# A third of the K of `h @ w_out` as seven block products, in a kernel of windowed attention and two gated layers

## The chip, the cores and the metric

One core of one Trainium2 chip. The metric is device time of one execution in microseconds (us); lower is better.

## What is computed

```
scores = q @ k.T / sqrt(64), masked to 0 <= row - col < 64; x = softmax(scores) @ v
h   = silu(x @ w_gate) * (x @ w_val)
x2  = h @ w_out
out = ((x2 @ w1) * (x2 @ w2)) @ w3 @ w_out2
```

q, k, v have 4 batches, 8 heads, 576 rows and 64 columns; x is taken as 2304 tokens of 512. w_gate and w_val are 512x1536, w_out 1536x512, w1 and w2 512x1024, w3 1024x1024, w_out2 1024x512. All of it is fp32. The results of attention feed the first gated layer, and so on to the end: it is one chain.

## The kernel before

**Words and passes.** Every fp32 operand is split into a high word and the rest (`cast` makes the first, `rest` the second), and every product is made in three passes over the words: high by high, high by low, low by high (`PASSES`). One matmul takes a weight tile of 128x128 and 384 token columns.

**Stages.** TensorE (PE) works through attention, the first gated layer (36 units), the projection by w_out (`project`, matmuls at L834), the second gated layer, and last the product with w3 and w_out2, which are multiplied with each other on the way. The 2304 tokens are three parts (`tp`) of 768, each in two halves of 384 columns.

**A gated unit** (`Unit.product`) makes one 256-column group (`fp`) of one weight (x = 0: gate, x = 1: value) for one token part as seven block products in place of eight: sums of the operands' blocks are made first, and sums of the products afterwards. A product is 6 matmuls. The banks of PSUM that it goes through are named `al`, `ga`, `be`; in a trace their names end in a and b for x = 0 and 1, and the operand words are `xo` (first layer) and `xp` (second). DVE makes the sums (`add`, `combine`, L681, L231) and the rests (L227), ACT the copies out of PSUM (L377) and the casts (L218), and the finished group of h goes to HBM as `h`.

**The projection** is the plain product: for each token part 12 tiles of K, and for each of them 4 tiles of output columns, 2 token halves and 3 passes, 288 matmuls. The 8 sums (4 by 2) stay in the 8 banks of PSUM (`o`). Nothing but the words of h (`pl` and `ph`, loaded back from HBM by `Rows.queue` 384 KB at a time, then cast and rest) and the resident tiles of w_out (`wo`) is waited for. In the last tile of K each bank is evicted as it is done (`evict`, on ACT L377 and L817, on DVE L820). ACT and DVE also narrow and split weights that are needed later (`st_z`, `st_w`, `st_a`: `narrow`, L194 to L207), and SP writes their words to HBM (`zd`, `w3d`).

**The order on the other engines.** A planner (`Plan`) writes it while the kernel is built. Work is a `Job` with a rank, a due number, costs and a lag; `fill` puts into an engine's stream whatever could start by its reckoning, `need` puts a job there because the next matmul reads it. What stands in a stream is done in that order: an instruction that waits holds up all that stands behind it on its engine. All loads of the projection are issued by SP, and eight DMA semaphores go round, so each DMA waits for the eighth before it.

## Time and profile before

| | |
|---|---|
| median of 3 runs | 825.1 us (824.4 to 825.12) |
| profiled execution, span | 822.8 us |
| PE busy | 811.8 us |
| the projection | from 362.02 to 511.78 us of the span |

The profile is of one execution, and shows its span, from the first instruction to the last; the page gives no other time for that execution. The median lies 2.3 us above the span, which is what a run has around the instructions. Busy time of PE is a sum over the pipelined matmuls; whether it stands still is read from its waits and from the distance of matmul starts, not from the busy share.

### The profile page before, as it was taken

The numbers are of one execution on the slowest core, as the hardware profiler recorded it, in microseconds if no ns is written. First come the engines' busy times: TensorE is split into PE (matmuls) and PEld (weight loads), VectorE is DVE, ScalarE is ACT, GpSimd is POOL, SyncE is SP. The second block draws the span as 40 slices with busy tenths as digits, with TensorE's granted clock in tenths as the row PEclk, the third lists the DMA queues.
The fourth block names the chain that finished last, engine by engine and source line by source line (L and its number), as shares of the span: only waits on it lengthen the run. The fifth ranks groups of instructions, "written<-read, shape, count | busy, mean of one in ns | idle before, by whom it ended". The sixth has DMA issues, their size and how long they took to land.

```text
span 822.8 us, 15571 instructions
## 1 busy us (share of the span) xinstructions
PE 811.8 (99%) x5702; PEld 783.5 (95%) x5702; DVE 637.4 (77%) x1353; ACT 455.1 (55%) x1194; POOL 90.8 (11%) x135
## 2 busy tenths in 40 slices
PE   7999999999999999999999999999999999999998
PEld 5777899999999999999999999999999998899997
DVE  5899898686887959866888683877888844789994
ACT  6899997555556445633663551444444423655543
POOL 3666842000000000000000000000010110000000
PEclk9999999999999999999999999999999999999999
DMA  9999295253562444599987712024565289107632
GB/s 187 195 200 197 46 238 113 90 192 129 192 222 79 148 154 179 210 360 403 373 264 175 231 57 103 29 83 134 166 205 157 108 295 325 37 3 207 182 71 78
DMA packets 172765, 140.23 MB, mean 170 GB/s; under 512 B 120848, under 2 KB 142608, under 8 KB 171664
## 3 DMA queue, kind: packets, MB, share of 16 engines
q1 hardware_dynamic: 167888, 125.86, 50.6%
q0 software_dynamic: 4800, 13.37, 5.9%
q8 instruction: 45, 0.74, 0.4%
q14 instruction: 32, 0.26, 0.1%
HBM read 92.27 MB, written 42.99 MB: 164 GB/s over the span
## 4 chain that ended last, share of the span: by engine, by line
PE 91%; ACT 4%; SPq 2%; DMA 2%; DVE 1%; issue 0%; POOL 0%; ACTq 0%
PE o L834 18%; PE ala L669 15%; PE alb L669 15%; PE bea L669 8%; PE beb L669 8%; PE acc L992 5%; PE al L1135 4%; PE gaa L669 4%; PE gab L669 4%; ACT pexp L480 2%; PE be L1135 2%; PE al L1067 2%; PE PV L519 1%; SPq L403 1%; PE be L1067 1%; PE ga L1135 1%
## 5 line engine op out<-in xcount | busy, mean ns | idle before, releaser
L834 PE MATMUL o<-ph,wo 128*128 128x384 f32 x576 | 146.2, 334 | 0.0
L834 PEld LDWEIGHTS o<-ph,wo 128*128 128x128 f32 x576 | 103.9, 188 | 0.0
L834 PE MATMUL o<-pl,wo 128*128 128x384 f32 x288 | 96.2, 334 | 0.0
L377 ACT ACTIVATE ha<-ala 128x384 f32<-128x384 f32 x102 | 49.5, 489 | 50.1 <-PE ala L669 49.5
L759 POOL DMA_DIRECT2D h<-ha x24 | 13.0, 544 | 548.2 <-DVE ha L691 548.2
L681 DVE TENSOR_TENSOR ha<-ha,bea 128x384 f32<-128x384 f32 x60 | 33.1, 551 | 38.5 <-PE bea L669 22.1
L834 PEld LDWEIGHTS o<-pl,wo 128*128 128x128 f32 x288 | 54.1, 188 | 0.0
L480 ACT ACTIVATE pexp<-S,stat 128x128 f32<-128x128 f32 x144 | 53.3, 428 | 0.0
L218 ACT CAST hf<-h 128x384 fp32r<-128x384 f32 x84 | 38.7, 514 | 14.4 <-DVE h L231 13.6
L694 ACT ACTIVATE ha<-ha 128x384 f32<-128x384 f32 x54 | 28.3, 526 | 32.4 <-DVE ha L681 32.4
L227 DVE TENSOR_TENSOR hf<-h,hf 128x384 fp32r<-128x384 f32 x84 | 42.2, 545 | 4.9 <-ACT hf L218 4.8
L227 DVE TENSOR_TENSOR pl<-pl,ph 128x768 fp32r<-128x768 f32 x36 | 33.4, 953 | 13.2 <-ACT ph L218 12.8
L218 ACT CAST ph<-pl 128x768 fp32r<-128x768 f32 x36 | 29.2, 837 | 25.1 <-DMA pl<-h 22.6
L490 POOL TENSOR_TENSOR pexp<-pexp,stat 128x384 f32<-128x384 f32 x48 | 39.0, 833 | 36.4 <-DVE stat L487 18.0
L377 ACT ACTIVATE c12b<-alb 128x384 f32<-128x384 f32 x30 | 14.8, 493 | 50.3 <-PE alb L669 50.0
L480 ACT ACTIVATION_READ_ACCUMULATOR pexp<-S,stat 128x1 f32 x144 | 38.1, 267 | 0.0
L681 DVE TENSOR_TENSOR c22b<-c22b,beb 128x384 f32<-128x384 f32 x30 | 16.6, 553 | 25.8 <-ACT c22b L377 25.8
L669 PE MATMUL ala<-xo,w_g_7h 128*128 128x384 f32 x120 | 30.3, 336 | 0.5 <-ACT ha L377 0.5
L473 DVE TENSOR_REDUCE stat<-S 128x3 f32<-128x384 f32 x48 | 24.4, 550 | 7.6 <-PE S L466 7.4
L669 PE MATMUL ala<-xo,w_g_1h 128*128 128x384 f32 x126 | 29.2, 335 | 0.0
L218 ACT CAST xp<-X 128x384 fp32r<-128x384 f32 x42 | 19.7, 519 | 10.9 <-DVE X L231 8.0
L377 ACT ACTIVATE c11b<-alb 128x384 f32<-128x384 f32 x30 | 14.7, 489 | 19.5 <-PE alb L669 19.5
(625 smaller groups left out, 2453.2 us busy)
## 6 DMA issues: line engine op xcount, KB each, us to landing
h<-ha SPq DMA_DIRECT2D x36, 384.0 KB, 3.0
pl<-h SPq DMA_DIRECT2D x36, 384.0 KB, 6.3
h<-ha POOLq DMA_DIRECT2D x24, 384.0 KB, 3.2
h<-h SPq DMA_DIRECT2D x24, 384.0 KB, 6.4
st_w<-in_moe_w_dram SPq DMA_DIRECT2D x8, 1024.0 KB, 6.5
st_wo<-in_moe_w_out_dram SPq DMA_DIRECT2D x6, 1024.0 KB, 5.1
wo<-by_wo SPq DMA_DIRECT2D x12, 512.0 KB, 4.1
st_g<-in_moe_w_gate_dram SPq DMA_DIRECT2D x5, 1024.0 KB, 5.2
```

The lines of the kernel that those rows point to most:

```text
L218: (eng.copy if eng is nc.scalar else eng.tensor_copy)(out=hi(), in_=src())
L227: return plan.job(lambda eng: eng.tensor_tensor(out=lo(), in0=src(), in1=hi().bitcast(F32), op=ALU.subtract), after, slots=slots, due=due, ...
L377: nc.scalar.mul(out=out, in_=in_, mul=-1.0)
L480: nc.scalar.activation(out=pe[:, jj, :], in_=so[:, jj, :], func=AF.Exp, bias=st[:, 0, x, jj:jj + 1], accum_out=st[:, 1, x, jj:jj + 1])
L490: nc.gpsimd.tensor_tensor(out=pe, in0=pe, in1=st[:, 3, x, :].unsqueeze(2).to_broadcast([P, SUB, P]), op=ALU.mult)
L669: nc.tensor.matmul(acc, lhsT=self.wt.ops[p, x][:, m, :], rhs=self.xs.ops[p, m][:, y, :], start=start and n == 0, stop=n == 5, skip_group_c ...
L681: nc.vector.tensor_tensor(out=out, in0=x, in1=y, op=ALU.add)
L694: nc.scalar.activation(out=h, in_=src, func=func, scale=-1.0 if direct else 1.0)
L834: nc.tensor.matmul(acc[m, x], lhsT=wos.tiles[i // 6][:, i % 6, :], rhs=rows[2 * tp + x].words(f, b), start=f == n == 0, stop=f == NF - 1 a ...
L992: nc.tensor.matmul(acc, lhsT=w3T[i][c // 3][:, x, (c % 3) * P:(c % 3) * P + P], rhs=zt[c, y], start=c == k == 0, stop=c == NI - 1 and k == 2)
L1067: nc.tensor.matmul(acc, lhsT=self.xs.ops[p, m][:, x, t * P:t * P + P], rhs=right.ops[p, m, y], start=start and n == 0, stop=n == 3 * R - 1 ...
L1135: nc.tensor.matmul(acc, lhsT=right.ops[p, m, y][:, P * k:P * k + P], rhs=self.xs.ops[p, m][:, x, :], start=bool(name) and n == 0, stop=n = ...
```

## The change

**Seven products for a third of K.** In the projection the K groups 0 and 1 (512 of 1536) are taken as a 2x2 block product with seven products (`SEVEN`, `STEPS`), the other four groups stay plain. Per token part that is 7 x 2 x 2 x 3 = 84 matmuls in place of 96, and 276 in place of 288. The seven come first in each part. Their banks are used again inside the part: after product 1 ACT copies `al` to `ga` (`seed`), after product 6 it copies `al` out, after product 7 it copies `al` to `de`; the plain groups then add onto `al`, `be`, `ga` and `de`.

**The operands of the seven.** The sums of h are made by DVE at the end of the units of value groups 0 and 1 (`spread`: four adds, and six stores by SP in place of two). Those of w_out are made in the class `Seven` (seven operands for each group). The projection loads 15 pairs of rows for each part in place of 12, and w_out lies in 20 resident tiles in place of 16.

**With it.** From the seventh unit on, gated units copy the first product into the bank of the second one, which adds onto it (`AT_SEEDED`): one DVE add less per unit. `narrow` handles weights that come in one load in pieces of 1024 columns in place of two of 512. The planner gets counts of rows, due numbers for loads, and shorter lags; the pool `half` has 5 buffers in place of 7, `sl` 58 in place of 56.

```diff
+AT_SEEDED = {1: 0, 5: 2, 2: 3, 6: 4, 7: 8, 4: 12, 3: 13}
...
@@ -137,7 +145,7 @@
                     for j in self.queue:
                         if e not in j.cost or (j.early and e == "DVE" and not self.early) or any(x.done is None for x in j.after):
                             continue
-                        if j.slots and self.slots < j.slots + self.keep:
+                        if j.slots and self.slots < j.slots + self.keep or j.rows and (self.rows[j.rows] < 1 or j.behind and j.behind.done is None):
                             continue
                         at = max([t] + [x.done for x in j.after])
...
 
-        n = 512
         a = plan.job(lambda eng: eng.tensor_scalar(out=low(), in0=low(), scalar1=29, scalar2=None,
                                                    op0=ALU.logical_shift_right), [load], due=due,
...
+    def cast(hi, src, after, n, slots=1, negate=False, due=0.0, rows=0):
         def fn(eng):
             if negate and eng is nc.scalar:
...
+            if self.second is None:
+                return [narrow(lambda: self.st, self.loaded[0], self.due, 1024)] * 2
+            return [narrow(lambda j=j: self.st[:, 512 * j:512 * j + 512], self.loaded[j], self.due, 512) for j in range(2)]
 
         def make(self):
             pass
...
+    SEEDED = 6
+    SEVEN = (0, 1)
+    stored = {}
...
+                elif (i, t) == (0, 0) and self.seeded:
+                    nc.scalar.copy(out=h, in_=src)
+                    plan.charge("ACT", act(T))
 
...
+
+
+                    self.seeded = self.n >= SEEDED
+                    if self.seeded:
+                        self.ga = bank(f"ga{self.name}")[:, :T]
+                    self.c11 = self.ga if self.seeded else self.own(0, 0, "c11")
                     later(1, lambda: self.copy(self.c11, self.al))
+                elif p == 2 and self.seeded:
+                    plan.wait(self.read)
+                    self.mm(self.ga, 2)
+                    self.put(0, 0, self.ga)
                 elif p == 2:
-                    ga = bank(f"ga{self.name}")[:, :T]
-                    self.mm(ga, 2, True)
-                    self.add(self.c11, self.c11, ga)
+                    self.ga = bank(f"ga{self.name}")[:, :T]
+                    self.mm(self.ga, 2, True)
+                    self.add(self.c11, self.c11, self.ga)
...
-                            store(out=hd[self.fp, self.tp][:, i, :], in_=t)
-                        plan.slots += 2
+                        h = hs.pop((self.fp, self.tp))
+                        if func != AF.Copy and self.fp in SEVEN:
+                            spread(self.fp, self.tp, h)
+                        else:
+                            for i, t in enumerate(h):
+                                store(out=hd[self.fp, self.tp][:, i, :], in_=t)
+                            plan.slots += 2
+                            done = mark()
+                            done.done = plan.charge("DVE", 0.0) + 4.0
+                            stored[self.fp, self.tp] = [done]
...
+    H_AT = {1: 0, 5: 1, 2: 2, 3: 3, 6: 4, 7: 5, 4: 6}
...
+    def spread(fp, tp, h):
+
+
+        to, f = h7d[tp], SEVEN.index(fp)
+        keep, plan.rank = plan.rank, SPREAD_RANK
+        (h00, h01), (h10, h11) = ((t[:, :T], t[:, T:]) for t in h)
...
+        first = put((1,), lambda: h00, [now])
+        both = put((2, 3), lambda: h[1].rearrange("p (c t) -> p c t", c=2), [now])
+        extra = []
+
+        def apart():
+            extra.append(small([P, T], F32, f"hs{fp}_{tp}"))
+            return extra[0]
+        s7 = combine(apart, lambda: h01, lambda: h11, ALU.add, [now], T)
+        s5 = combine(lambda: h01, lambda: h01, lambda: h00, ALU.add, [s7], T)
+        s6 = combine(lambda: h11, lambda: h11, lambda: h01, ALU.add, [s5, both], T)
+        s4 = combine(lambda: h10, lambda: h10, lambda: h11, ALU.add, [s6], T)
+        p5 = put((5,), lambda: h01, [s5])
+        put((7,), lambda: extra[0], [s7])
+        put((6,), lambda: h11, [s6])
+        p4 = put((4,), lambda: h10, [s4])
+        plan.job(gone, [first, p5, s6], SP=0.0)
+        plan.job(gone, [p4], SP=0.0)
+        plan.rank = keep
+
+
...
 
...
-                eng.dma_start(out=self.lo[fp].bitcast(F32), in_=self.hd[fp, self.tp][:, :, T * self.x:T * self.x + T])
+                self.lo[key] = slot([P, 2, T], F32R, f"pl{self.tp}_{key[0]}_{key[1]}", False)
+                f, x = key
+                eng.dma_start(out=self.lo[key].bitcast(F32),
+                              in_=h7d[self.tp][:, H_AT[f]] if x == 7 else h1d[f, self.tp][:, :, T * x:T * x + T])
 
             def hi():
-                self.hi[fp] = slot([P, 2, T], F32R, f"{self.name}h{self.tp}_{self.x}_{fp}")
-                return self.hi[fp]
-            a = loading(load, after, 2)
-            b = cast(hi, lambda: self.lo[fp].bitcast(F32), [a], 2 * T)
-            self.jobs[fp] = rest(lambda: self.lo[fp], lambda: self.lo[fp].bitcast(F32), lambda: self.hi[fp], [b], 2 * T)
-
-        def words(self, f, x):
-            return (self.lo if x else self.hi)[f // 2][:, f % 2, :]
+                self.hi[key] = slot([P, 2, T], F32R, f"ph{self.tp}_{key[0]}_{key[1]}", False)
+                return self.hi[key]
+            a = loading(load, stored[key[0], self.tp, 7] if key[1] == 7 else stored[key[0], self.tp], rows=1, lag=7.0, due=due)
...
+    STEPS = (1, 5, 6, 2, 7, 3, 4)
...
-            acc = {(m, x): bank(f"o{tp}_{m}_{x}")[:, :T] for m in range(NM) for x in range(2)}
-
-            def evict(m, x):
-
-
-                dst = x2[m][:, T * x:T * x + T]
-                if x or tp == 0:
...
+            al, ga, be, de = ([None] * 2 for _ in range(4))
+            r = rows[tp]
+
+            def open_bank(to, m, name):
+                to[m] = bank(f"{name}{tp}_{m}")[:, :T]
+
+            def seed(to, src, m, name):
+                open_bank(to, m, name)
+                nc.scalar.copy(out=to[m], in_=src[m])
+                plan.charge("ACT", act(T))
...
+            def copy(r, c, src, m):
+                (negated if r == c else nc.scalar.copy)(out=part(r, c, m), in_=src[m])
+                plan.charge("ACT", act(T))
+
+            def add(r, c, src, op, m):
+                nc.vector.tensor_tensor(out=part(r, c, m), in0=part(r, c, m), in1=src[m], op=op)
+                plan.charge("DVE", dve(T))
+
+            def product(acc, key, w, g, m, start=False, stop=False):
+                plan.need(r.jobs[key])
+                for n, (x, y) in enumerate(PASSES):
+                    plan.need(wos.job(w, g, x, m))
+                    nc.tensor.matmul(acc, lhsT=wos.words(w, g, x, m), rhs=r.words(key, g, y),
+                                     start=start and n == 0, stop=stop and n == 2, skip_group_check=not start)
...
+            for k, p in enumerate(STEPS):
+                for event in events.get((tp, k), ()):
...
+                to = {2: ga, 5: be, 3: be}.get(p, al)
+                for m in range(2):
+                    if p in (1, 5):
+                        open_bank(to, m, "al" if p == 1 else "be")
+                    for g in range(2):
+                        product(to[m], (p, 7), p, g, m, p in (1, 5) and g == 0, True)
+                    if p == 1:
+                        seed(ga, al, m, "ga")
+                    elif p == 5:
+                        copy(1, 1, be, m)
+                    elif p == 6:
+                        copy(0, 1, al, m)
+                    elif p == 7:
+                        seed(de, al, m, "de")
+                    if m:
...
+            for k, fp in enumerate(plain):
+                for event in events.get((tp, len(STEPS) + k), ()):
+                    event()
+                for g in range(2):
+                    last = g == 1 and fp == plain[-1]
+                    for b, (i, c, to) in enumerate(((1, 0, al), (0, 1, be), (0, 0, ga), (1, 1, de))):
+                        for m in range(2):
+                            product(to[m], (fp, c), (fp, i), g, m, False, last)
+                            if last:
+                                if (i, c) == (1, 0):
+                                    copy(1, 0, al, m)
+                                elif (i, c) == (0, 1):
+                                    add(0, 1, be, ALU.add, m)
+                                elif (i, c) == (0, 0):
+                                    copy(0, 0, ga, m)
+                                else:
+                                    add(1, 1, de, ALU.subtract, m)
+                        if b == 1 or b == 3:
...
+            xop2[tp] = Operands([lambda x=x: x for x in x2], f"xp{tp}", dict.fromkeys(PRODUCTS, opened), X2_SUMS, X2_RESTS, due=14.0 * tp)
...
+    class Seven(Doubles):
+
+
+        GROUPS = ((1, 2), (5, 6), (7, 3), (4,))
+
+        def __init__(self, src, n):
+            super().__init__(src[256 * n:256 * n + 256, :].rearrange("(j p) f -> p j f", p=P), f"wo{n}")
...
+
+                def put(eng, group=group, t=t):
+                    for q, p in enumerate(group):
+                        eng.dma_start(out=w7d[p][:, SEVEN.index(self.n)], in_=t[0][:, q].rearrange("p x f -> p (x f)").bitcast(F32))
+                by.append(plan.job(put, jobs, lag=5.0, SP=0.5 * len(group)))
+                for p in group:
+                    self.stored[p] = by[-1]
...
+    on(events1, last1 - 2, lambda: (make_to(wo[-1]), weight_loads(0, 4)))
+    on(events1, last1 - 1, lambda: (share(), project_loads(0), weight_loads(4, 7)))
+    on(events1, last1, lambda: weight_loads(7, 9))
     events_p = {}
-    on(events_p, (0, 0), lambda: (setattr(plan, "landing", 10.0), make_to(w3s[NW3 - 1])))
+    on(events_p, (0, 0), lambda: (setattr(plan, "landing", 8.0), setattr(plan, "keep", 0), make_to(w3s[NW3 - 1])))
+    for n in range(3):
+        on(events_p, (0, 2 * n), lambda n=n: weight_loads(9 + 2 * n, 11 + 2 * n))
+    on(events_p, (0, 7), lambda: project_loads(1))
+    on(events_p, (1, 7), lambda: project_loads(2))
+    opened = mark()
+    X2_SUMS, X2_RESTS = (), ()
...
```

**How it moves instructions, 1: DVE in the first gated layer, at the end of the unit of value group 0, first token part (about 123 us in the trace of before).** `X2_0` and `X2_1` hold columns of x of the third token part, `xo2_50` to `xo2_61` its operand words for products 5 and 6, `ha` and `c11b`, `c22b` the sums of the units, `st_g1` a weight that is narrowed. Before:

```order
L691 TENSOR_TENSOR ha0_1_0_2330<-ha0_1_0_2330,c11b0_1_2428 128x384
L227 TENSOR_TENSOR xo2_50_2462<-X2_0_1540,xo2_50_2462 128x384
L227 TENSOR_TENSOR xo2_51_2472<-X2_1_1632,xo2_51_2472 128x384
L231 TENSOR_TENSOR X2_0_1540<-X2_0_1540,X2_2_1794 128x384
L231 TENSOR_TENSOR X2_1_1632<-X2_1_1632,X2_3_1879 128x384
L681 TENSOR_TENSOR ha0_1_0_2330<-ha0_1_0_2330,bea0_1_2374 128x384
L194 TENSOR_SCALAR st_g1_2253<-st_g1_2253 128x512
L227 TENSOR_TENSOR xo2_60_2506<-X2_0_1540,xo2_60_2506 128x384
L227 TENSOR_TENSOR xo2_61_2509<-X2_1_1632,xo2_61_2509 128x384
```

Now, from the third of the four added sums of h (`ha0_0_1`) on:

```order
L238 TENSOR_TENSOR ha0_0_1_2125<-ha0_0_1_2125,ha0_0_0_2124 128x384
L238 TENSOR_TENSOR X2_1_1642<-X2_1_1642 128x384
L238 TENSOR_TENSOR ha0_0_1_2125<-ha0_0_1_2125 128x384
L695 TENSOR_TENSOR ha0_1_0_2340<-ha0_1_0_2340,bea0_1_2384 128x384
L201 TENSOR_SCALAR st_g1_2263<-st_g1_2263 128x1024
L234 TENSOR_TENSOR xo2_50_2519<-X2_0_1550,xo2_50_2519 128x384
L234 TENSOR_TENSOR xo2_51_2522<-X2_1_1642,xo2_51_2522 128x384
L238 TENSOR_TENSOR X2_0_1550<-X2_0_1550,X2_2_1804 128x384
L695 TENSOR_TENSOR c22b0_1_2543<-c22b0_1_2543,beb0_1_2477 128x384
L702 SCALAR_TENSOR_TENSOR ha0_1_1_2341<-c22b0_1_2543,ha0_1_1_2341 128x384
L695 TENSOR_TENSOR ha0_2_0_2525<-ha0_2_0_2525,gaa0_2_2550 128x384
L234 TENSOR_TENSOR xo2_60_2559<-X2_0_1550,xo2_60_2559 128x384
```

The words `xo2_50` and `xo2_51` stood ahead of the add to `ha0_1_0` and of the narrowing; now they stand behind both, and the narrowing is twice as wide. `xo2_60` has moved behind three instructions of the units (`c22b`, `ha0_1_1`, `ha0_2_0`) that stood behind it. The sum that makes `X2_1` stood ahead of `xo2_60`; it now follows right behind the last row, and `xo2_61` behind it.

**2: ACT at the change from the first to the second token part of the projection (about 412 us).** `X2` are the results that leave PSUM, `ph1` the high words of the second part's rows, `st_w30` and `st_w31` pieces of w3. Before:

```order
L203 ACTIVATE st_w30_5228<-st_w30_5228 128x512 x2
L377 ACTIVATE X2_0_0_4932<-o0_0_0_4936 128x384
L817 COPY X2_0_0_4932<-o0_0_1_4937 128x384
L377 ACTIVATE X2_0_1_4933<-o0_1_0_4938 128x384
L817 COPY X2_0_1_4933<-o0_1_1_4939 128x384
L817 COPY X2_0_2_4934<-o0_2_0_4940 128x384
L377 ACTIVATE X2_0_2_4934<-o0_2_1_4941 128x384
L817 COPY X2_0_3_4935<-o0_3_0_4942 128x384
L377 ACTIVATE X2_0_3_4935<-o0_3_1_4943 128x384
L218 CAST ph1_0_1_5387<-pl1_0_1_5297 128x768
```

Now:

```order
L225 CAST ph1_6_7_5311<-pl1_6_7_5241 128x768
L225 CAST ph1_2_7_5317<-pl1_2_7_5243 128x768
L210 ACTIVATE st_w30_5224<-st_w30_5224 128x1024
L908 COPY X2_0_2_4932<-al0_0_4934 128x384
L908 COPY X2_0_3_4933<-al0_1_4953 128x384
L387 ACTIVATE X2_0_0_4930<-ga0_0_4941 128x384
L387 ACTIVATE X2_0_1_4931<-ga0_1_4960 128x384
L225 CAST ph1_7_7_5393<-pl1_7_7_5313 128x768
L225 CAST ph1_3_7_5397<-pl1_3_7_5315 128x768
L210 ACTIVATE st_w31_5295<-st_w31_5295 128x1024
L901 COPY ga1_0_5416<-al1_0_5409 128x384
L901 COPY ga1_1_5426<-al1_1_5419 128x384
```

The copies out of the banks stood behind the scaling of `st_w30`, with the casts of rows behind them; now two casts of rows stand ahead of it too, and the seeds `ga1` behind two more casts and the scaling of `st_w31`.

## Rows read from the trace of the kernel before

**Rows 1.** Page, part 1: span, then busy us of the engines

```profile
span 822.8 us, 15571 instructions
...
PE 811.8 (99%) x5702; PEld 783.5 (95%) x5702; DVE 637.4 (77%) x1353; ACT 455.1 (55%) x1194; POOL 90.8 (11%) x135
```

**Rows 2.** Waits of PE, longest first: waited for, us, times, longest

```profile
PE pm L563 <- POOL masks L553: 2.1, 1, 2.1
...
PE ala L669 <- ACT ha L377: 0.5, 1, 0.5
```

**Rows 3.** Page, part 5: the groups of line L834, busy us and mean ns

```profile
L834 PE MATMUL o<-ph,wo 128*128 128x384 f32 x576 | 146.2, 334 | 0.0
...
L834 PE MATMUL o<-pl,wo 128*128 128x384 f32 x288 | 96.2, 334 | 0.0
```

**Rows 4.** Timeline of PE, both ends of the projection: start, duration, instruction

```profile
362.02 0.33 PE L834 MATMUL o<-ph,wo 128*128 128x384 f32 x1
...
511.60 0.33 PE L834 MATMUL o<-ph,wo 128*128 128x384 f32 x1
511.78 1.20 PE L669 MATMUL ala<-xp,w_a_1h 128*128 128x384 f32 x6
```

**Rows 5.** Timeline of DVE around the unit of group 0, third token part

```profile
124.00 1.02 DVE L227 TENSOR_TENSOR xo<-X,xo 128x384 fp32r<-128x384 f32 x2
124.94 1.01 DVE L231 TENSOR_TENSOR X<-X,X 128x384 f32<-128x384 f32 x2
126.13 0.55 DVE L681 TENSOR_TENSOR ha<-ha,bea 128x384 f32<-128x384 f32 x1 [0.18 <-PE bea L669]
126.61 0.42 DVE L194 TENSOR_SCALAR st_g<-st_g 128x512 int32<-128x512 int32 x1
126.94 1.02 DVE L227 TENSOR_TENSOR xo<-X,xo 128x384 fp32r<-128x384 f32 x2
127.88 0.68 DVE L197 SCALAR_TENSOR_TENSOR st_g<-st_g 128x512 int32<-128x512 int32 x1
```

**Rows 6.** Timeline of PE, products five and six of that unit

```profile
129.06 1.20 PE L669 MATMUL bea<-xo,w_g_2l 128*128 128x384 f32 x6
130.10 1.20 PE L669 MATMUL ala<-xo,w_g_4h 128*128 128x384 f32 x6
```

**Rows 7.** Busy us by stretch: PE, PEld, DVE, ACT, POOL, clock, DMA share, GB/s

```profile
100.00:130.00 30.00, 29.52 (x187) 28.45 (x186) 27.96 (x63) 27.51 (x67) 16.17 (x19) 1.00 1.03 217
362.00:412.00 50.00, 50.00 (x291) 50.00 (x290) 34.96 (x55) 23.46 (x37) 0.00 (x0) 1.00 1.03 389
412.00:462.00 50.00, 50.00 (x290) 50.00 (x289) 36.58 (x62) 21.56 (x38) 0.00 (x0) 1.00 0.79 211
```

**Rows 8.** Timeline of ACT at the first change of token part

```profile
408.58 1.29 ACT L203 ACTIVATE st_w<-st_w 128x512 f32<-128x512 f32 x2 [2.44 <-DVE st_w L197]
409.77 0.47 ACT L377 ACTIVATE X<-o 128x384 f32<-128x384 f32 x1
```

**Rows 9.** Timeline of SP, DMA issues ahead of the first and second change

```profile
398.38 0.42 SPq L263 DMA_DIRECT2D st_w<-in_moe_w_dram  x1
...
407.14 0.64 SPq L263 DMA_DIRECT2D st_w<-in_moe_w_dram  x1
...
448.48 0.51 SPq L263 DMA_DIRECT2D st_a<-in_moe_w_dram  x1
...
450.76 8.88 SPq L1227 DMA_DIRECT2D w3d<-by_w  x8
```

**Rows 10.** Page, part 6: DMA issues, KB each, median us to landing

```profile
pl<-h SPq DMA_DIRECT2D x36, 384.0 KB, 6.3
...
st_w<-in_moe_w_dram SPq DMA_DIRECT2D x8, 1024.0 KB, 6.5
```

**Rows 11.** ACT in the projection: groups by line, busy us, mean ns, idle before

```profile
L218 ACT CAST ph<-pl 128x768 fp32r<-128x768 f32 x34 | 27.6, 837 | 25.1 <-DMA pl<-h 22.6 <-PE o L834 2.3
...
L817 ACT COPY X<-o 128x384 f32<-128x384 f32 x8 | 3.8, 490 | 22.7 <-PE o L834 22.7
```

240 lines of the change are left out of this document (155 added, 85 removed).

## The prediction

> **What bounds the kernel now.** I read the page's busy times first: PE is busy 811.8 of 822.8 us [rows 1], and DVE, the next, 77%. A busy share cannot tell whether PE stands still, so the waits of PE come second: the longest is 2.1 us and belongs to attention, and the only one that a unit of the first gated layer has is 0.5 us [rows 2]. Third, the projection: its 864 matmuls [rows 3] start at 362.02 and the next stage at 511.78 us [rows 4], 149.76 / 864 = 0.1733 us each, with no gap. So PE's own work sets the end, and a matmul less is worth 0.1733 us as long as nothing makes PE wait. The question is what the change makes late. For that the tables of stretches show two places with little room: DVE is busy 27.96 of 30 us just ahead of 130 us, and the DMA engines are full (share 1.03, 389 GB/s) in the first 50 us of the projection [rows 7].
>
> **What the change takes off PE.** Twelve matmuls for each of three token parts, 36 in all: 36 x 0.1733 = **-6.24 us**. The words, tile sizes and column counts stay, so I keep the price of one. The seeded gated units give PE the same 42 matmuls in another order: 0.
>
> **What it adds elsewhere.** (1) DVE in the first gated layer, first and second row of order shown above. PE reads the words `xo2_60` and `xo2_61` in the product that starts at 130.10 us [rows 6]; before, DVE had them ready at 126.94 + 1.02 = 127.96, 2.1 us ahead [rows 5]. Now four more sums stand ahead. Two neighbours of this size start 0.47 us apart (the pair at 124.00, the next at 124.94), so the new ones cost 1.9 us; but the add at 126.13 waits for PE in any case (its releaser), and takes up what piles up ahead of it. I walk on from there: the narrowing starts at 126.61 and lasts 0.42 at 512 columns; twice as wide I take 0.6, between 0.42 and two times 0.42. Then come two rests and a sum (3 x 0.47, to 128.6), three instructions of the units that stood behind these before (0.47, 0.58, 0.47, to 130.1), the rest of `xo2_60` (0.55), the sum for `X2_1` (to 131.1), a cast on ACT of 0.5, and the rest of `xo2_61`: 132.2. PE reads that in its fifth matmul of the product, 130.10 + 4 x 0.17 = 130.8. It waits about 1.5 us. Another 0.3 for the last operand words of this token part, which stand behind the same sums: **+1.8**. From below it is 0.5 (if the unit's three instructions run as early as their products allow), from above 3.0 (a second such place as dear as the first, where the sums of the second part fall).
>
> (2) The first change of token part. Before, each of eight sums had its own bank, and ACT needed only to be done with a bank when the next part's product came to it. Now `al` is written by products 1, 6, 7 and 4 of the same part, with ACT reading in between, so a copy that stands behind a cast, which waits for a load, stops PE. At the change (362.02 + 288 x 0.1733 = 411.9, call it 0) I use the load times of before. The first piece of w3 was issued at 398.38 [rows 9] and its scaling was over at 409.87 [rows 8], so the two copies of `al` behind it would be done at about -1.2, which is in time: 0. The second piece was issued at 407.14, -4.8; it lands 6.5 us later [rows 10], at +1.7. Two narrowing steps follow (0.6, and 1.2 for 1024 columns where 512 take 0.68 [rows 5]), then a scaling as long as the two halves of before (1.29 [rows 8]), to +4.7, and the seed of `ga` (0.4): +5.1. Product 6 writes onto `al` as the third product, 24 matmuls in: +4.2. So PE waits about **+1.0**. The two casts of rows ahead of it (0.84 each [rows 11]) run meanwhile. Bounds: 0 if the piece is issued 1 us earlier; 2.9 if it takes from issue to scaling as long as the first (398.38 to 408.58, 10.2 us), which ends the chain at +7.1.
>
> (3) The second change. Two casts of rows and six casts of w1's words now stand ahead of the copies of `al`. Before, that piece of w1 was issued at 448.48, 13.4 us ahead of the change at 461.9, and eight writes of w3 followed, from 450.76 on for 8.9 us [rows 9]. If the rows are issued behind half of those (4.4 us), at -6.7, they land at -0.4 [rows 10], and two casts (1.7) and six (2.2) put the copy at about +4. In the changed order the last two pieces of w3 stand well ahead of where they stood, in the middle of the part, so I take **0**, and 4 as the other end.
>
> (4) The start of the projection. Three more pairs of rows (1.15 MB) for the first part fall into the stretch with full DMA engines; at 389 GB/s [rows 7] that is 3.0 us. The seven's rows exist long before the stage starts and most are loaded ahead of it, so I take **+0.3**, from 0 to 3.0.
>
> (5) Hidden: nine casts (9 x 0.84 = 7.5 us) and nine rests more, and the seeds, in 143.5 us of projection, where ACT is busy 23.5 of 50 us and DVE 35 to 37 [rows 7]; without that cover they would be part of (2) and (3). Fewer adds in the seeded units relieve DVE in a stretch where PE waits for nothing: 0. Of SP's added stores and loads I charge only their place ahead of others, in (1) to (4).
>
> **The sum:** -6.24 + 1.8 + 1.0 + 0 + 0.3 = -3.1 us. The profiled execution's span is 822.8, which becomes 819.7; the median lies 2.3 above it, 825.1, so I forecast **822.0 us**.
>
> **The rivals.** A, nothing waits: all added work finds room, 825.1 - 6.2 = 818.9. For it: in all of the first gated layer PE waits 0.5 us for ACT and has no wait for DVE worth a row, although DVE is busy 27.96 of 30 us in it [rows 2, 7]. Against it: 2.1 us of lead at (1) against some 4 us of work that has been put in front.
>
> B, the other side: ACT's order becomes the bound where the token part changes. ACT waited 22.6 us for row loads in the projection [rows 11]; before, that held up nobody, now a bank's copy or seed stands behind such a cast. The price is the upper ends of (2) and (3), 2.9 + 4.1 = 7.0 in place of 1.0: 822.0 + 6.0 = 828.0. It decides from where the loads land some 2 us later, against the change of part, than they did. For it: the eviction at 409.77 already stood behind a scaling that had waited 2.44 us for DVE [rows 8]. Against it: between ACT's read of `al` and the next product onto it lie 18 to 24 matmuls, 3.1 to 4.2 us, and a copy takes 0.49 [rows 11]. The Trainium skill (Perfetto Trace Analysis, Optimizing Tensor Performance, Matmuls) asks that independent groups of matmuls rotate through different banks, so that evacuating one overlaps the next; the change goes against that, since one bank takes four products in a row. By that rule each of the six reads of `al` in the midst of a part would be exposed, and the time would be near B. The units of the first layer already use `al` so, and their one wait for ACT is the 0.5 us of [rows 2]; to that extent the trace speaks against the rule.
>
> C, the start of the projection is bound by DMA: +3.0 in place of 0.3, 822.0 + 2.7 = 824.7, no change that could be told. For it the share of 1.03; against it, that PE did not wait there before.
>
> **How the numbers follow.** About 0.2% (1.65 us) is what a measurement of this kernel can tell from no change. The forecast has a chance of 0.50 (faster in nine of ten of its outcomes, else the same), A 0.22, B 0.16, C 0.12. Faster: 0.45 + 0.22 + 0.02 = 0.69; the same: 0.05 + 0.08 + 0.02 = 0.15; slower: 0.14 + 0.02 = 0.16. The range goes from A, less 0.3, to 826.5: it takes in C and the smaller half of B; the upper half of B and a little on both sides is left out.
>
> **What would show it.** Right: 5090 matmuls at 0.1733 us, the projection some 145 us long, PE waits for DVE (`xo`) of 1 to 2 us near 130 us, and one for ACT at the start of the second token part. A is seen by no new row among PE's waits; B by waits for ACT of `al` of several us at both changes of part; C by waits for rows or for `wo` just behind 362 us. I am wrong in kind if matmuls onto seeded banks start further apart than 0.1733 us, or if PE waits in a place that none of (1) to (4) names.

## The result, and the profile after

The changed kernel takes 835.48 us (median of 4, 834.58 to 837.48) against 825.11 us before on the same chip: a ratio of 1.0124, 95% interval 1.0108 to 1.014. It is **10.4 us slower**; 822.0 was forecast. The profiled execution's span is 832.8 us, before 822.8 [rows 1].

The page of the changed kernel, parts 1, 5 and 6:

```profile
span 832.8 us, 15558 instructions
...
PE 814.2 (98%) x5666; PEld 780.7 (94%) x5666; DVE 635.2 (76%) x1252; ACT 470.7 (57%) x1206; POOL 92.8 (11%) x135
...
L919 PE MATMUL al<-ph,wo 128*128 128x384 f32 x192 | 55.7, 343 | 3.6 <-ACT de L901 3.1
...
L225 ACT CAST ph<-pl 128x768 fp32r<-128x768 f32 x45 | 37.4, 835 | 29.9 <-DMA pl<-h 29.3
...
pl<-h SPq DMA_DIRECT2D x45, 384.0 KB, 6.9
```

There are 36 matmuls fewer (5666 records, 5702 before), and yet PE is busy longer; the `al` group's mean of 343 ns says that some of its matmuls were slower than the 334 of before. ACT waits 29.3 us for loads of rows where it waited 22.6 [rows 11], and these loads take 6.9 us from issue to landing instead of 6.3 [rows 10]. The waits of PE, where the first gated layer had one of 0.5 us [rows 2]:

```profile
PE al L919 <- ACT de L901: 3.1, 2, 1.9
...
PE alb L683 <- ACT c12b L387: 1.9, 1, 1.9
...
PE gaa L683 <- ACT gaa L387: 1.7, 1, 1.7
PE ala L683 <- DVE xo L234: 1.2, 2, 1.0
...
PE al L919 <- ACT ga L901: 0.5, 1, 0.5
```

PE's timeline at the two ends of the projection, at one place in it and near 130 us:

```profile
129.43 0.44 PE L683 MATMUL ala<-xo,w_g_4h 128*128 128x384 f32 x1
130.87 0.62 PE L683 MATMUL ala<-xo,w_g_4h 128*128 128x384 f32 x2 [1.00 <-DVE xo L234]
131.88 0.44 PE L683 MATMUL ala<-xo,w_g_4h 128*128 128x384 f32 x1 [0.39 <-ACT xo L225]
...
371.95 0.33 PE L919 MATMUL al<-ph,wo 128*128 128x384 f32 x1
...
434.37 0.34 PE L919 MATMUL be<-ph,wo 128*128 128x384 f32 x1
436.61 0.44 PE L919 MATMUL al<-ph,wo 128*128 128x384 f32 x1 [1.90 <-ACT de L901]
...
437.09 0.84 PE L919 MATMUL al<-ph,wo 128*128 128x384 f32 x2
437.73 0.53 PE L919 MATMUL al<-pl,wo 128*128 128x384 f32 x1
...
521.50 0.51 PE L683 MATMUL ala<-xp,w_a_1h 128*128 128x384 f32 x2
```

The projection starts at 371.95 instead of 362.02 us (9.93 later) and ends at 521.50 instead of 511.78 [rows 4]. It should have become 6.24 us shorter and lasts 149.55 instead of 149.76. So there are two losses: some 9.9 us ahead of it and 6.0 us inside it. To find them I go along PE's timeline and take, wherever the next record starts later than the last one's start plus 0.1733 us a matmul, the difference. What comes out:

| at (us) | lost | PE waits for | what stood ahead of it |
|---|---|---|---|
| 129.4 to 132.5 | 2.35 | `xo`, words from DVE and ACT | sums of h on DVE |
| 133.3 to 136.5 | 1.47 | nothing | lower clock: 10 matmuls in 3.20 us |
| 205.6 | 1.88 | seed of `ga` from ACT | a silu that waits 4.03 us for DVE |
| 212.5 | 0.54 | value weights of group 2 | their late load |
| 364.8 to 369.8 | 2.57 | `c12b`, `c22b` from ACT | three casts of rows, 0.83 us each, that wait 1.42 us for loads; two more |
| 385.3 | 1.39 | seed of `de` from ACT | a cast that waits 2.95 us for a load |
| 425.3 | 0.65 | seed of `ga` from ACT | two casts that wait 1.90 us for loads, a scaling |
| 434.4 | 2.07 | seed of `de` from ACT | a cast that waits 2.66 us for a load |
| 437.1 to 440.5 | 1.53 | nothing | lower clock: 11 matmuls in 3.44 us |

Together 14.45 us. To be found are 10.0 + 6.24, and 1.3 more: attention, which the change doesn't touch, happens to end at 100.40 us in this execution and at 101.69 in the one before (over all the runs below its end lies between 100.2 and 102.8). The other 3.1 us lie in pieces of under 0.3 us. Some of the lines in detail. ACT, behind a wait for DVE and behind loads of rows (start, duration, instruction, idle time before it and what ended it):

```profile
206.72 0.52 ACT L708 ACTIVATE ha<-ha 128x384 f32<-128x384 f32 x1 [4.03 <-DVE ha L695]
207.16 0.47 ACT L387 ACTIVATE gaa<-ala 128x384 f32<-128x384 f32 x1
...
363.78 0.83 ACT L225 CAST ph<-pl 128x768 fp32r<-128x768 f32 x1 [1.12 <-DMA pl<-h]
...
366.48 0.48 ACT L387 ACTIVATE c12b<-alb 128x384 f32<-128x384 f32 x1
...
385.59 0.83 ACT L225 CAST ph<-pl 128x768 fp32r<-128x768 f32 x1 [2.95 <-DMA pl<-h]
386.33 0.47 ACT L901 COPY de<-al 128x384 f32<-128x384 f32 x1
...
422.84 1.77 ACT L225 CAST ph<-pl 128x768 fp32r<-128x768 f32 x2 [1.90 <-DMA pl<-h]
...
435.35 0.83 ACT L225 CAST ph<-pl 128x768 fp32r<-128x768 f32 x1 [2.66 <-DMA pl<-h]
436.08 0.85 ACT L901 COPY de<-al 128x384 f32<-128x384 f32 x2
```

The seeds take 0.47 us each (207.16, 386.33; the line at 436.08 shows two in 0.85); most of the time is in the idle time of the instruction ahead. DVE, which ACT waited for at 206.72, and SP, which had issued that load late:

```profile
203.76 0.69 DVE L201 TENSOR_SCALAR st_v<-st_v 128x1024 int32<-128x1024 int32 x1 [2.67 <-DMA st_v<-in_moe_w_val_dram]
205.67 0.56 DVE L238 TENSOR_TENSOR ha<-ha,ha 128x384 f32<-128x384 f32 x1 [1.21 <-DMA h<-ha]
```

```profile
192.99 0.38 SPq L270 DMA_DIRECT2D st_wo<-in_moe_w_out_dram  x1
...
194.45 0.95 SPq L270 DMA_DIRECT2D st_v<-in_moe_w_val_dram  x1
```

DVE stands 2.67 us behind the load of the value weights of group 2, issued at 194.45 us, and 1.21 us behind a store of h. In the kernel before that load was issued at 170.55 us, ahead of w_out's second group; now it comes behind it, as w_out's first group, loaded at 149 us, keeps one of the two load buffers until its seven sums are made at 193 us.

### The profile page after: what moved, and what is told of

Read it like the earlier page. It is cut to its first block, busy times and chain, and to the rows that moved or that the text cites. A ratio compares the mean times of both kernels' runs of the same rounds, so it can differ in the third digit from the quotient of the medians.

```text
span 832.8 us, 15558 instructions
## 1 busy us (share of the span) xinstructions
PE 814.2 (98%) x5666; PEld 780.7 (94%) x5666; DVE 635.2 (76%) x1252; ACT 470.7 (57%) x1206; POOL 92.8 (11%) x135
## 4 chain that ended last, share of the span: by engine, by line
PE 84%; DMA 8%; DVE 3%; ACT 2%; issue 1%; SPq 1%; POOL 0%; ACTq 0%; POOLq 0%; DVEq 0%
PE alb L683 14%; PE ala L683 13%; PE beb L683 7%; PE bea L683 6%; PE acc L1116 5%; PE al L1259 4%; PE al L919 4%; DMA pl<-h 4%; PE gab L683 3%; PE gaa L683 3%; PE be L919 3%; PE PV L529 2%; PE S L476 2%; PE ga L919 2%; PE PT L509 2%; PE T L439 2%
## 5 line engine op out<-in xcount | busy, mean ns | idle before, releaser
L789 POOL DMA_DIRECT2D h<-ha x24 | 13.6, 570 | 553.9 <-DVE ha L705 553.9
L919 PE MATMUL al<-ph,wo 128*128 128x384 f32 x192 | 55.7, 343 | 3.6 <-ACT de L901 3.1
L234 DVE TENSOR_TENSOR pl<-pl,ph 128x768 fp32r<-128x768 f32 x45 | 42.4, 955 | 19.2 <-ACT ph L225 18.9
L225 ACT CAST ph<-pl 128x768 fp32r<-128x768 f32 x45 | 37.4, 835 | 29.9 <-DMA pl<-h 29.3
L387 ACT ACTIVATE ha<-ala 128x384 f32<-128x384 f32 x78 | 38.0, 489 | 25.6 <-PE ala L683 25.0
L919 PE MATMUL be<-ph,wo 128*128 128x384 f32 x144 | 41.4, 334 | 0.0
L919 PEld LDWEIGHTS al<-ph,wo 128*128 128x128 f32 x192 | 36.2, 193 | 4.6 <-ACT de L901 3.8
L919 PE MATMUL ga<-ph,wo 128*128 128x384 f32 x120 | 34.8, 334 | 0.0
L919 PE MATMUL al<-pl,wo 128*128 128x384 f32 x96 | 32.7, 341 | 0.0
L919 PE MATMUL de<-ph,wo 128*128 128x384 f32 x96 | 28.2, 334 | 0.0
L702 DVE SCALAR_TENSOR_TENSOR ha<-alb,ha 128x384 f32<-128x384 f32 x30 | 16.6, 553 | 14.9 <-PE alb L683 14.6
```

Source lines behind the costliest of these rows:

```text
L225: (eng.copy if eng is nc.scalar else eng.tensor_copy)(out=hi(), in_=src())
L234: return plan.job(lambda eng: eng.tensor_tensor(out=lo(), in0=src(), in1=hi().bitcast(F32), op=ALU.subtract), after, slots=slots, due=due, ...
L387: nc.scalar.mul(out=out, in_=in_, mul=-1.0)
L919: nc.tensor.matmul(acc, lhsT=wos.words(w, g, x, m), rhs=r.words(key, g, y), start=start and n == 0, stop=stop and n == 2, skip_group_check ...
```

## The experiments

Every kernel is compared with the kernel before on the same chip; "+x" is the difference of the two medians. The changed kernel is at +10.4. Two theories. **Order:** PE waits because what it needs on ACT or DVE stands in their queues behind something that waits for a DMA; other orders of the same work cure it. **Amount:** VectorE's sums of h (24 of 0.55 us, one 0.47 us behind the other) are too much for the first layer in any order.

**Rows counted on later.** The order of work is fixed when the program is built; a load of rows is taken to be there 7.0 us after its issue.

```diff
-            a = loading(load, ..., rows=1, lag=7.0, due=due)
+            a = loading(load, ..., rows=1, lag=9.0, due=due)
```

> The planner reckons 9 us in place of 7 for a load of rows, so the casts of rows stand later in ACT's stream; nothing else is changed. Theory 1, order: ACT's copies and seeds no longer stand behind casts that wait for their load, and the losses at 365 us (2.7) and in the projection (5.8 with the lower clock) fall to under 4 us together: 830.5 to 832. Rival, the loads come too late whatever the order (10 MB more in all): PE then waits for rows, 834.5 to 836.5.

Measured 831.02 us, +7.2 (ratio 1.0083, 1.0067 to 1.01), 3.2 us less than the changed kernel, as the theory had it. Not all of that is the edit's. From the end of attention to the end of the projection the profiled execution is 3.9 us shorter; 2.1 of these arise ahead of 361 us, where the order on ACT and DVE is the same in both kernels: the stops at 129 us lose 1.7 us in place of 2.35, and the clock doesn't fall behind them. 0.8 us are gained at 365 us and 1.0 in the projection (148.57 us). There the stops at 385, 425 and 434 us go or shrink, and a new one of 2.7 us comes at 417 us, where sums that leave PSUM stand on DVE behind a narrowing of w3, which waits 0.99 us for its load, and behind two rests, with 1.5 us at a lower clock after it. So order moves these stops, but this one number does not yet cure them.

**The casts of rows on GpSimd.**

```diff
...
-            b = cast(hi, lambda: self.lo[key].bitcast(F32), [a], 2 * T, 0, rows=2, due=due)
+            b = plan.job(lambda eng: eng.tensor_copy(out=hi(), in_=self.lo[key].bitcast(F32)), [a], rows=2, due=due, ROWS=pool(2 * T))
```

> The 45 casts of rows are done by GpSimd, which is idle there, so ACT has no instruction left in the projection that waits for a load of rows; loads, rests and PE's order stay as planned. Theory 1, order: PE's waits for ACT at 365 us and in the projection go, 8.5 us less: 826.5 to 829 (a slower cast may give back a little). Rival, the loads are late: the waits become waits for rows, 834 to 837.

834.4 us, +10.6 (1.0126, 1.0107 to 1.0144): no gain, and so not the theory; the profile is of the fastest of its four executions, 831.03 us. The waits behind casts at 365 and 385 us go, but PE loses 1.6 us at 384 us for the words of rows themselves, from GpSimd and DVE, and 1.6, 1.7 and 1.1 us at 417, 428 and 473 us. At 417 us the sums that leave PSUM stand on DVE behind a narrowing and a rest, at 428 us ACT's copy of `al` behind a scaling that waits 3.61 us for DVE. Taking the casts off ACT is not enough while other work stands in the way on both.

**The sums of h behind the weights**, the other way round in DVE's queue:

```diff
-    SPREAD_RANK = 0
+    SPREAD_RANK = 2
```

> The four sums of h (spread) get a lower rank than the operand words xo, so they stand behind them on VectorE. Theory 1, order: PE loses time because what it needs stands in a stream behind instructions that are not urgent or that wait for a DMA. Then the two waits for xo near 130 us (2.5 us lost, and 1.6 at the lower clock behind them) go: 831 to 832.5 us against 835.5. Rival, too much work: VectorE and the DMA engines have more to do than fits, so the loss only moves: 834.5 to 836.5.

836.87 us, +13.1 (1.0155, 1.0133 to 1.0176), a little above the rival too. The wait at 130 us falls to 0.5, and 3.9 us for weights appear at 206 to 211 us. A loss that moves speaks for amount, but does not show it: this is one other order.

**Units without seeds.** The adds on VectorE come back in all units.

```diff
...
-    SEEDED = 6
+    SEEDED = 1000
```

> The gated units as before: no copy of the first product into the bank of the second, the add on VectorE is back. Theory 1, order: the 1.9 us wait at 206 us has its cause in VectorE's stream, which waits for a load of w_val and a store of h, so most of it stays or moves to the next reader of al: 834 to 835.5. Rival, the seeds cost: the wait goes, and others like it at 332 us, so 832 to 833.5.

860.73 us, +36.9 (1.0444, 1.0424 to 1.0463), far from theory and rival, with stops of up to 7.1 us for weights. It tells less than was meant: unseeded units need more of the small buffers, of which the change left five for seven; that this is the cause of the 36.9 us is likely and not shown. The same part by itself, in the kernel before (seven buffers):

```diff
-        when = [(7 * n + AT[p], n, p) for ...
+        when = [(7 * n + (AT_SEEDED if n >= SEEDED else AT)[p], n, p) for ...
...
+                elif p == 2 and self.seeded:
+                    plan.wait(self.read)
+                    self.mm(self.ga, 2)
+                    self.put(0, 0, self.ga)
```

> The kernel before with one part of the change alone: from the seventh unit on the product of the fifth sum runs before that of the second, the first product is copied by ScalarE into the second product's bank, and the add on VectorE is left out. No products in blocks of seven, no sums of h, 2048 matmuls-worth of projection as before, seven half buffers as before. Theory (the seeds themselves cost nothing where VectorE has air; the loss comes with the sums and the rows): 823.5 to 826, same as before. Rival (the seeds put ScalarE ahead of TensorE in each unit and cost by themselves): 828 or more, with waits of ga or al for ScalarE in each unit. Third case (VectorE was a hidden bound before): 822.5 or less.

824.92 us, +0.4 (1.0001, 0.999 to 1.0013). Stretches of this kernel (columns as in [rows 7]), with the same one of the kernel before in the second fence:

```profile
200.00:362.00 162.00, 162.00 (x936) 161.82 (x935) 113.61 (x237) 87.03 (x187) 0.00 (x0) 1.00 0.49 175
```

```profile
200.00:362.00 162.00, 162.00 (x936) 162.00 (x935) 124.71 (x259) 86.56 (x188) 0.00 (x0) 1.00 0.49 176
```

The seeds take 11 us off VectorE from 200 to 362 us and give nothing, since PE waits for nothing there. They cost nothing that the medians show either, some 1.1 us at most by the interval; the loss is elsewhere. (The projection that this kernel keeps has 864 matmuls, not 2048 as the expectation says.)

**Stores of the sums and of w_out's sevenths on GpSimd's queue; then with the later rows too.**

```diff
-                         after, lag=4.0, SP=0.5)
+                         after, lag=4.0, DMA=1.0)
...
-                by.append(plan.job(put, jobs, lag=5.0, SP=0.5 * len(group)))
+                by.append(plan.job(put, jobs, lag=5.0, DMA=1.0 * len(group)))
```

> The stores of the sums of h (36) and of w_out's seven operands (14) are issued by GpSimd's queue in place of SP's; nothing else is changed. Theory 2, SP's queue: each such store waits on SP for VectorE's sum and for a semaphore, and the loads of weights stand behind it (w_val's third group was issued at 194.5 us, 170.6 before), so VectorE and ACT wait for the load and PE for them. Then that load is issued before 180 us, the 1.9 and 0.9 us at 206 to 214 us go, and the late starts of the projection's loads shrink: 830 to 832.5 us. Rival, VectorE has too much to do: the issue time changes and the waits of PE stay, 834.5 to 836.5.

> The stores on GpSimd's queue, and 9 us in place of 7 for a load of rows. If the two causes are separate, the gains add (4.5 of the second alone, 3 to 5 of the first): 826 to 828.5 us. If both act on the same waits: 830 to 831.

833.15 us, +8.9 (1.0101, 1.0086 to 1.0116), and with both 829.82 us, +5.6 (1.0061, 1.0038 to 1.0084). The first lies between theory and rival; the two gains, 1.5 and 3.2 us, add up to what both give (4.8), though each is smaller than was taken. The waits at 205 to 214 us go and 1.4 us come at 251 us. Yet the load of the value weights is issued as late as in the changed kernel:

```profile
193.44 0.37 SPq L270 DMA_DIRECT2D st_v<-in_moe_w_val_dram  x1
```

So stores ahead of it on SP were not what held it. And a load at 193 us need not cost anything at 205: here DVE starts on it at 200.48 us without a wait, where in the changed kernel it stood 2.67 us until 203.76, and no sum of h waits for a store.

**Further turns of the order** on top of that: the sums between xo and the weights, and then z's stores on GpSimd too.

```diff
-    SPREAD_RANK = 0
+    SPREAD_RANK = 1
```

> As the one before, and the sums of h behind the operand words of x on VectorE. Theory 2: late sums now hold up no load, so the waits near 130 us go without the 3.9 us for w_val's words that followed when they stood on SP's queue: 822 to 825. Rival, VectorE has too much to do: those 3.9 us come again, 826 to 830.

```diff
-        eng.dma_start(out=zd[f], in_=t.bitcast(F32))
+        nc.gpsimd.dma_start(out=zd[f], in_=t.bitcast(F32))
```

> As the one before, and the eight stores of w_out2's words (zd) in the projection on GpSimd's queue too. Theory 2: the loads of w3 behind them on SP start earlier, and the waits of PE at the changes of token part (2.5 us with 9 us of lag) shrink by 1 to 2 us: 820.5 to 823.5. Rival: no difference within 1 us to the one before.

838.08 us, +13.9 (1.016, 1.0144 to 1.0177), and 841.42 us, +17.2 (1.021, 1.0191 to 1.023), both worse than theory and rival: 4.6 us are lost for value weights at 211 us, and in the second 5.6 us at a token part's end besides. In these three ranks, what stands last is late.

**The loads of w_out's groups**, meant to go back to where they stood before the change:

```diff
-        if at[1] < len(coming) and (coming[at[1]] in wo or isinstance(coming[at[1]], Plain)):
-            coming[at[1]].due = coming[at[1] - 1].due + 7.0
-            make_to(coming[at[1]], rank, ahead)
```

> The change, but each group of w_out is again loaded and queued together with the next group of weights, as before the change, and not right behind the weights ahead of it. In the changed kernel the value weights of group 2 are loaded at 194 us instead of 171 us, because a group of w_out takes one of the two load buffers first. Theory (order: the loss at 205 to 214 us comes from that late load): the waits there, 1.88 and 0.86 us, go, the rest stays; 831.5 to 833.5. Rival (VectorE has too much to do in the first gated layer, so what is early for one weight is late for another): the wait moves to another weight or another sum, 834 to 838.

856.13 us, +31.6 (1.0397, 1.0367 to 1.0428), worse than theory and rival. Waits of PE in this kernel:

```profile
PE ala L683 <- ACT w_g_1h L225: 9.1, 1, 9.1
PE al L919 <- ACT X L908: 7.6, 1, 7.6
PE alb L683 <- ACT w_v_1h L225: 6.0, 1, 6.0
```

The edit did not do what it was meant to: w_out's first and second group are loaded at 148.51 and 192.18 us, still ahead of the value weights of group 2, which come later yet (202.10 us). The same edit with the stores and later rows:

> The same with the two edits that helped before: the stores of the sums of h on GpSimd's queue, and rows counted on 9.0 us after their load is issued. Theory (order): the 1.4 us at 251 us goes as well, the 2.2 us at 130 us and the waits at the borders of the token parts stay; 827 to 829. Rival (too much work for VectorE): no better than with the loads in the changed order, 829.8 or above.

858.23 us, +33.7 (1.0422, 1.0396 to 1.0449). These two runs do not test the late load. They show that without the early making of w_out's groups this order loses 21 us more.

**Seven sums made of later groups**, where VectorE has more room:

```diff
-    SEVEN = (0, 1)
+    SEVEN = (2, 3)
```

> The change with one number pair altered: the products in blocks of seven are made of the third and fourth group of h and w_out instead of the first and second. The same sums, stores, casts and products, some 60 us later in the first gated layer, where VectorE is busy 72% of the time (117.14 of 162 us from 200 to 362 us) instead of 88% (130 to 200 us and before it). Theory (order and place: the losses at 129 to 136 us and at 205 to 214 us, some 6.9 us in all, come from the sums and from the first group of w_out holding a load buffer from 149 to 193 us, in the stretch with the least room): they go and nothing takes their place, the 8.8 us at 365 us and in the projection stay; 827.5 to 829.5. Rival (the added work of the first layer is too much wherever it lies): waits of the same size come at 215 to 300 us; 834 to 838.

847.85 us, +23.2 (1.028, 1.0253 to 1.0307), worse than theory and rival. No stop over 0.9 us is left between 100 and 290 us, but:

```profile
PE alb L683 <- ACT w_v_1h L225: 10.2, 2, 8.1
PE al L919 <- ACT de L901: 7.5, 2, 6.4
```

8.1 of those 10.2 us lie at 333 us, for the last value weights, whose load is issued at 325.35 us; in the changed kernel it was issued at 317.88. The wait has moved with the sums and has grown, though VectorE has room there: fullness near 130 us is not all. A late load is, as at 205 us, the likely way. With the stores and later rows on top, the same groups and then the fourth and fifth:

> The third and fourth group, with the two edits that helped before: the stores of the sums and of w_out's seven products on GpSimd's queue, and rows counted on 9.0 us after their load. Theory: the gains add up, as 2.2 us at 130 us and 1.4 us at 251 us of the 829.82 go; 825 to 827.5. Rival: 829 or more, with waits for weights at 215 to 300 us.

> As before but the fourth and fifth group, later still. Theory: the first layer is as free of waits, but the last sums lie nearer to the rows' first loads, so it ends no better than with the third and fourth: 825 to 829. Rival: 829 or more, with waits in the first layer at 260 to 340 us.

838.27 us, +13.6 (1.0165, 1.0138 to 1.0193), and 840.96 us, +16.3 (1.0197, 1.0177 to 1.0216), both as the rival had it in time, with 3.9 and 4.9 us for the last value weights at 331 to 337 us; for the third and fourth group the rival had looked for that at 215 to 300 us.

**The seven sums in one rank with the weights**, so that the buffer comes free sooner:

```diff
-            plan.rank = rank if rank is not None else 1 if isinstance(coming[at[1]], Weights) else 2
+            plan.rank = rank if rank is not None else 1 if isinstance(coming[at[1]], (Weights, Seven)) else 2
```

> The change, but the making of the seven sums of w_out's first two groups stands in one rank with the weights (by due time), not behind all of them. So the load buffer that the first group holds from 149 to 193 us in the changed kernel comes free some 20 us sooner, and the value weights of group 2 are loaded ahead of w_out's second group instead of behind it. Theory (the loss at 205 to 214 us is the load buffer that is held too long): the 1.88 and 0.86 us there go, with no wait for weights in their place; 831.5 to 833.5. Rival (VectorE has no room for the sums before 200 us, so what is made sooner makes something else late): a wait of some 2 to 5 us for a weight or xo between 150 and 260 us; 834.5 to 839.

834.85 us, +10.6 (1.0131, 1.0109 to 1.0153). SP's loads:

```profile
171.04 0.38 SPq L270 DMA_DIRECT2D st_g<-in_moe_w_gate_dram  x1
...
175.52 0.46 SPq L270 DMA_DIRECT2D st_v<-in_moe_w_val_dram  x1
...
199.08 0.47 SPq L270 DMA_DIRECT2D st_wo<-in_moe_w_out_dram  x1
```

The value weights are loaded at 175.52 us, 19 us sooner, and the stops at 205 to 214 us are gone. Together with the stores on GpSimd's queue, where the load was late and the stops went too, this points to two things that made them, the held buffer being one: it seems to take the late load, and an order on DVE in which a sum of h that waits for a store stands behind the work on that load. But 1.1 us at 192 us and 1.8 us at 233 us, both for gate weights, take their place, as the rival said. With the two edits:

> The same with the stores on GpSimd's queue and rows counted on 9.0 us after their load (829.82 us so far). Theory: the 1.4 us at 251 us goes; the 2.2 us at 130 us and the waits at the borders of the token parts stay; 827.5 to 829. Rival: 830 or more.

831.46 us, +7.2 (1.0095, 1.0074 to 1.0116): the rival again.

**The additions left out:** what the sums cost by themselves.

```diff
...
-        s7 = combine(apart, lambda: h01, lambda: h11, ALU.add, [now], T)
-        s5 = combine(lambda: h01, lambda: h01, lambda: h00, ALU.add, [s7], T)
-        s6 = combine(lambda: h11, lambda: h11, lambda: h01, ALU.add, [s5, both], T)
-        s4 = combine(lambda: h10, lambda: h10, lambda: h11, ALU.add, [s6], T)
+        s7 = s5 = s6 = s4 = now
...
```

> The change without the 24 additions on VectorE that make the four sums of h (24 of 0.55 us): the blocks are stored as they are in the places of the sums, so that the products of the third of K are taken of unsummed blocks. Stores, loads, casts and all matmuls stay. It prices the sums alone. Theory (order: the sums cost because of where they stand, between xo and the weights before 215 us, and the projection's waits have another cause): the losses at 129 to 136 and 205 to 214 us, 6.9 us together, go or shrink to under 2, the 8.8 us at 365 us and later stay; 828 to 831. Rival (the sums are not what fills VectorE there, the held load buffer and the stores are): 833 to 836.

827.87 us, +3.4 (1.0046, 1.0028 to 1.0065). Its waits of PE behind attention:

```profile
PE alb L683 <- ACT c12b L387: 2.3, 1, 2.3
...
PE al L911 <- ACT de L893: 1.9, 1, 1.9
PE al L911 <- ACT ga L893: 1.0, 1, 1.0
```

No wait for `xo` over 0.2 us, none for weights, none at 205 us; the load of the value weights is issued at 179.15 us, ahead of w_out's second group. The 24 sums cost 7.0 us (+10.4 less +3.4; by the two intervals some 2 us more or less), with all that hangs on them in this order. In the traces 5.1 us of it lie between the end of attention and the projection, where 6.2 were lost at 129 to 136 and at 205 to 214 us. 2.3 lie in the projection, which has no sums; there the clock doesn't fall in this execution (1.53 us). Stops behind casts of rows stay: 3.0 us at 361 to 366 us, 3.3 in the projection.

**Loads in the projection counted on later**, on top of the stores and later rows:

```diff
-    on(events_p, (0, 0), lambda: (setattr(plan, "landing", 8.0), ...
+    on(events_p, (0, 0), lambda: (setattr(plan, "landing", 11.0), ...
```

> The kernel with the stores on GpSimd's queue and rows counted on 9.0 us after their load (829.82 us), and one number more: while w_out is projected, the loads of weights for later are counted on 11.0 us after they are issued, not 8.0 (the load of w3 issued at 406.61 us in that kernel was ready for VectorE at 416.1, 9.5 us on). Theory (order): the wait of 3.4 us at 417 us, where the additions that end the first token part stand behind a narrowing that waits for such a load, gets under 1.5 us; 826.5 to 828.5. Rival (what is put later there is missed later): 829 or more, with the time lost at another border or at the end of the projection.

825.9 us against 824.52, +1.4 (1.0016, 1.0002 to 1.0029), better than either theory said, and still slower than the kernel before. Its stretches:

```profile
362.00:412.00 50.00, 48.09 (x274) 47.26 (x274) 33.38 (x41) 25.17 (x37) 0.00 (x0) 1.00 0.98 368
412.00:462.00 50.00, 50.00 (x291) 50.00 (x290) 37.33 (x45) 24.99 (x36) 0.00 (x0) 1.00 0.95 289
```

```profile
362.00:412.00 50.00, 46.53 (x266) 45.57 (x265) 35.27 (x43) 27.23 (x40) 0.00 (x0) 1.00 1.03 392
412.00:462.00 50.00, 47.62 (x264) 46.98 (x263) 35.32 (x44) 22.96 (x33) 0.00 (x0) 0.97 0.91 271
```

The first fence is this kernel, the second the changed one. From 412 us on PE runs without a gap; the projection goes from 369.03 to 513.60 us, 144.57 us where 143.5 is PE's own work. Up to 398 us its order on ACT and DVE is that of the kernel with 829.82 us, and its projection is 5.4 us shorter (149.94 there), so this gain lies where the edit is. It also answers the rival that the 10 MB of added transfers make the rows come too late in any order: all of them are still there. Three edits of order have taken 9 of the 10.4 us back, with all of the change's work in place. It still doesn't beat the kernel before: 2.3 us at 129 to 133 and 1.5 at the lower clock behind it, 1.8 at 249 to 256, 1.5 at 365 and 0.8 at 385 us are left, 7.9 in all, against 6.24 saved. This order without the sums wasn't tried.

## Why the prediction was wrong

- **The saving, -6.24: right.** The stretches without waits hold 302 matmuls in 52 us as before, seeded or not. (The 5090 matmuls at 0.1733 us that were to show it are miscounted: of the 5666, 4128 belong to the stages behind attention.)
- **(1) the sums at 130 us, +1.8: right place and cause, and a fair size.** PE loses 2.35 us there for the words of `xo`; in the runs with later rows and with the casts on GpSimd, whose order is the same up to there, it loses 1.7 and 2.0. It has no wait for DVE there in the run of the seeds alone. The lower clock behind it (1.47) was not in the sum.
- **The step that failed, by size: (5), which put the added casts and the seeds at nothing, "in 143.5 us of projection, where ACT is busy 23.5 of 50 us".** 7.97 us were lost where no term stood: the 6.05 of the projection and 2.57 ahead of it, less 0.65, which is (2). The losses are at 365 us, before the projection starts, and in the midst of parts (385, 434 us, with 1.53 at the lower clock behind), at the seed of `de`: an instruction of ACT that PE needs stands behind a cast that waits for a load. A busy share of ACT says nothing of what stands ahead of one instruction. That is the mechanism of rival B, but at places that it did not name, and it was given 0.16.
- **The second step that failed: (1) read VectorE's room at one place, 130 us, and "of SP's added stores and loads I charge only their place ahead of others, in (1) to (4)".** No term stood for 205 to 214 us, where 2.42 us are lost. The sums of h and w_out's seven sums also delay what frees a load buffer, and through it a load by 24 us, and DVE stands for that load and for a store. The run without the sums of h puts their whole price at 7.0 us, where (1) had 1.8, at most 3.0.
- **(2), the first change of part, +1.0: right place, 0.65 lost.** The seed of `ga` comes behind two casts and the scaling of w3's piece, as worked out; but the casts, which were to run meanwhile, waited 1.90 us for their loads.
- **(3), the second change of part, 0, and (4), the start of the projection, +0.3: right as far as they go.** PE loses nothing over 0.3 us at either place.
- **The sum again, from the trace:** -6.24 + 2.35 + 1.47 + 2.42 + 7.97 + 0.65 = +8.6 us; with 2.7 us in small pieces ahead of and behind the projection, less 1.3 for the shorter attention, the 10.0 us of the two spans.
- **Rival B's rule**, from the Trainium skill (Perfetto Trace Analysis, Optimizing Tensor Performance, Matmuls), that independent groups of matmuls rotate through banks so that evacuating one overlaps the next: by it each read of `al` in the midst of a part was to be exposed. In the last kernel above the banks are used just as in the changed one, and PE has no wait for `al` in the whole projection. What exposed the reads was the load ahead of them, and the trace doesn't bear out the rule as a price of its own here. The products onto `al` are also not independent of each other, since each adds onto what the ones before it left there, so the rule may not be meant for them.
- **A and C:** A fell. C is not seen: no wait for rows or `wo` just behind the start.
- **(5), the seeded gated units at 0: right**, by the run of the seeds alone.

What stays open: why the seven sums of w_out and the sums of h can't both be placed without a stop. For the projection order is shown to be the cause, as the last kernel has all of the work and hardly a wait there. For the first gated layer the orders tried moved the wait and none removed it, so between order and amount that stays undecided. That the stops at 129 us come from the sums is shown by the run without them; how the 7.0 us divide between DVE's time and the load buffer is argued, not shown.

## What to carry over

Where engines work through a fixed order, look for the price of added work in what waits behind a load on each queue, at every place where the engine that sets the end reads a result, not in busy shares, and not only at the borders of stages. A planner's assumed landing time is a tuning number of its own: here 2 us more of it for rows gave 3.2 us back, of which about half can be put down to it by the trace, and 3 us more for later weights another 4.2, which lie in the projection. And where a saving on the bounding engine needs new work on another, run it once with that work left out: the difference is the work's price in this order, and the rest has another cause. Last, before a gain is put down to an edit, compare the stretches that the edit doesn't touch: here two executions differed by 2 us in one of them.
